# Row sums and pooled products over 128 partitions in a fused attention and MLP kernel

## The chip, the cores and the metric

The kernel runs on one core of one Trainium2 chip. The metric is the device time of one execution in microseconds, the median of three timed runs. The profile comes from a further execution; its span, from the first to the last instruction, is a little shorter than the timed figure. TensorE is called PE, VectorE DVE, ScalarE ACT, GpSimd POOL; SP issues most of the DMA transfers.

## The reference, cut to what matters

Inputs q, k, v are 8 batches x 8 heads x 576 positions x 64 numbers in float32. Each head gets two attentions. One is local: a query sees only keys at a distance under four. The other is pooled: q, k and v are averaged over groups of four positions (144 groups), full attention is computed between groups, and each result is repeated four times. Their sum goes through an MLP.

```python
q_d = q.reshape(B, H, Sd, factor, D).mean(axis=3)      # likewise k_d, v_d; factor 4, Sd 144
out_up = np.repeat(sm_attn(q_d, k_d, v_d), factor, axis=2)
mask = np.abs(pos[:, None] - pos[None, :]) < factor
attn = softmax(np.where(mask, scale * q @ k.T, -1e9))
x = (out_up + attn @ v)                                # to 4608 x 512
h = x @ w_in                                           # 512 x 2048
out = (h * 1 / (1 + exp(-h))) @ w_out                  # 2048 x 512
```

## The kernel before

Heads are worked on in 32 pairs, head h of a pair on partitions 64h to 64h+63. The units of one pair are: T (36 transposes of q and k), S (scores into the PSUM banks AB), exponentials on ACT (Pt local, Pd pooled), Z (row sums by matmuls with 0/1 columns into columns 360 to 431 of the banks CD), a reciprocal on DVE, its spread over partitions (Rb), PV (products with v into CD), the multiplication of PV by Rb into xo, and an addition on POOL into xT. The MLP follows in g1 units (x by w_in, float32, four matmuls of 512 columns, tanh on ACT, a product on DVE) and g2 units (by w_out, bf16).

A list scheduler in the kernel with estimated costs decides the order in which each engine gets its units; a recorder then turns the order into instruction streams with semaphores. So a changed cost or priority can move instructions that the change doesn't touch.

Pairs 0 to 9 are issued as separate units, and for the first eight (NDIR) the reciprocals are spread by PE: split into three bf16 parts, each multiplied by a selector matrix (unit RB). The first eight (NVP) also get their pooled v by matmuls (unit VP); later ones by two POOL additions on an extra copy of v. From n = 10 on, one unit V(n) holds S(n), T(n+1), Z(n-1) and PV(n-2), followed by four g1 and four parts of a g2; there Rb goes through DRAM: scr is written from zr (z) and read back, repeated over 64 partitions (b), all issued from ACT.

```python
NVP = 8; NDIR = 8
# buffers of the first eight pairs lie in gT[1], which the MLP uses later
sel = gT[1][:, 0:2, :]...[:, 0:5, :]                   # 5 selectors 128 x 128
rpart = [gT[1][:, 2 + i, 0:144] for i in range(3)]
zr = sb("zr", [128, 2, 72], F32, 2)

def pe_S(u, p):                                        # 28 matmuls
    ...                                                # 20 local ones, 64x64
    for h in range(2):
        for y in range(2):
            mm(u, AB[half(y), h, 288:432], kd[j][half(h), 64 * y:64 * y + 64], qd[j][half(h), :], rd, [rAB[h]])
    for h in range(2):
        for y in range(2):
            mm(u, AB[half(y), h, 432:504], kd[j][half(h), 128:192], qd[j][half(h), 72 * y:72 * y + 72], rd, [rAB[h]])

def pe_VP(u, p):                                       # 14 matmuls, 64x64, two banks, one wait on itself
    ...

def pe_cross(u, pv, z):                                # products that cross the diagonal of the array
    if pv is not None:
        for h in range(2):
            for j in range(2):
                x = 1 - j
                mm(u, CD[half(h), x, 288:360], vd[n][half(j), 2 * h, :], Pd[m][half(j), h, 72 * x:72 * x + 72],
                   [...], [rCD[x], R(rc)], start=first(x, h), stop=False)
    if z is not None:
        ...                                            # four more, with oh4, into columns 360:432

def pe_main(u, pv, z):
    wait = [R(acc(z if pv is None else pv)[2])]        # the first matmul here waits for pe_cross
    if z is not None:
        for s in range(4):
            for h in range(2):
                for j in range(2):
                    mm(u, CD[half(h), j, 360:432], oh1[half(j), 63 - s:127 - s] if s else ohf[half(j), :],
                       Pt[m][half(j), h, 72 * s:72 * s + 72], [...], [rCD[j]], start=False, stop=False)
        ...                                            # 8 more, from Pd, with oh4 and ohc
    if pv is not None:
        ...                                            # 20 local products and 8 pooled ones, all 64x64

def after_Z(p):
    one("DVE", f"r{p}", 1.2, lambda e: e.reciprocal(zr[i][:, :, :], CD[:, :, 360:432]), r=rCD, ..., prio=-4)
    if p < NDIR:
        # rh on ACT, then rx (subtract), rm (cast), rl (subtract) on DVE: three bf16 parts of 144 columns
        ...
        return
    dma("ACT", f"z{p}", scr[u][:, :], zf, ...)         # 128 x 144 to DRAM
    for h in range(2):
        dma("ACT", f"b{p}", Rb[u][half(h), :], src, ..., r=[R(f"scr{u}")], prio=-5)

def RB(p):                                             # 18 matmuls: 6 column ranges x 3 parts
    for m, x, c, y, e_ in ((0, 0, 0, 0, 144), (1, 0, 144, 0, 144), (2, 0, 288, 0, 72),
                           (2, 1, 0, 72, 144), (3, 1, 72, 0, 144), (4, 1, 216, 0, 144)):
        for a in range(3):
            mm(u, AB[:, x, c:c + e_ - y], sel[:, m, :], rpart[a][:, y:e_], selr + [rpr[a]], [rAB[x]], ...)
    one("ACT", f"eb{p}", 0.85, ...)                    # AB to Rb

def V(n):
    pe_cross(u, pv, z)
    if n < NPAIR: pe_S(u, n)
    if n + 1 < NPAIR: pe_T(u, n + 1)
    pe_main(u, pv, z)
    ...

for n in range(10):
    T(n + 1); feed(); S(n)
    if n > 0: Z(n - 1)
    if n > 1: PV(n - 2); feed()
    if 0 < n <= NDIR: RB(n - 1); VP(n - 1)
    if n > 4: G1((2, 4, 4, 4, 2)[n - 5])
for n in range(10, 46):
    if n < NPAIR + 2: V(n); feed()
    G1(1); g2(part 0); G1(1); g2(part 1); G1(1); g2(part 2); g2(part 3); G1(1)
```

The code above is shortened, with cuts marked by dots and some lines joined.

Of the kernel before, what the change touches and what calls it, by code (L numbers as in the profile page):

```python
# [18 lines left out]
NVP = 8  # L19
NDIR = 8  # L20

# [127 lines left out]
class Unit:  # L149
# [3 lines left out]
                 "ready", "start", "end")  # L153
# [5 lines left out]


class Plan:
# [4 lines left out]
    def __init__(self):  # L166
        self.units = []

    def unit(self, eng, name, cost, prio=None, dcost=0.0):
        u = Unit(eng, name, cost, prio, dcost)  # L170
        u.idx = len(self.units)
        if u.prio is None:
            u.prio = u.idx
        self.units.append(u)
        return u
# [32 lines left out]
    def order(self, look):  # L208
# [12 lines left out]
        while left:  # L221
            best = None
            for e in Prog.ENGS:
                lst = pend[e]
                while head[e] < len(lst) and lst[head[e]] in taken:
                    head[e] += 1
                win = [u for u in lst[head[e]:head[e] + look[e]] if u not in taken and not u.npre]
                if not win:
                    continue
                t = max(free[e], min(u.ready for u in win))  # L230
                c = min((u for u in win if u.ready <= t + 0.05), key=lambda u: (u.prio, u.idx))
                t = max(t, c.ready)
                if best is None or t < best[0]:
                    best = (t, c)
            t, u = best
            u.start = t
            free[u.eng] = t + u.cost
            if u.dcost:
# [4 lines left out]
                u.end = ring[e] + 1.6  # L243
# [15 lines left out]
def bass_hourglass_attn__then__act_silu_kernel(  # L259
# [9 lines left out]
    with kctx:  # L269
# [34 lines left out]
        zr = sb("zr", [128, 2, 72], F32, 2)  # L304
        Rb = sb("Rb", [128, 720], F32, NR)
        xo = sb("xo", [128, 2, 360], F32, NX)
        scr = [nc.dram_tensor(f"scr{i}", [128, 144], F32, kind="Internal").ap() for i in range(NR)]

        sel = gT[1][:, 0:2, :].rearrange("p a (y m) -> p (a y) m", m=128)[:, 0:5, :]
        selr = [R("g1_0"), R("g1_1")]  # L310
        rpart = [gT[1][:, 2 + i, 0:144] for i in range(3)]
        rpr = [R(f"g1_{2 + i}") for i in range(3)]
        rrest = gT[1][:, 5, 0:288].bitcast(F32)
        idn = sb("idn", [128, 64], BF16)
        mask_bf = sb("mask_bf", [128, 288], BF16)
        oh1 = sb("oh1", [128, 127], BF16)
        ohf = sb("ohf", [128, 64], BF16)
        oh4 = sb("oh4", [128, 127], BF16)
        ohc = sb("ohc", [128, 127], BF16)
        pb = sb("pb", [128, 3, 136], BF16)  # L320
# [33 lines left out]
        def constants():  # L354
# [17 lines left out]
            for t, name, val in ((oh1, "oh1", 1.0), (oh4, "oh4", 4.0)):  # L372
                zero(t[:, :], name + "a")
                zero(t[:, 63:64], name, val, 0.07, r=[R(name + "a")])
            zero(ohf[:, :], "ohfa", 1.0)
            zero(ohf[:, 1:5], "ohf", 0.0, 0.07, r=[R("ohfa")])
            zero(ohc[:, :], "ohca")
            for j in range(2):
                zero(ohc[64 * j:64 * j + 16, 63:64], f"ohc{j}", 4.0, 0.07, r=[R("ohca")])
            zero(pb[:, :, :], "pba", cost=0.2)  # L380
            one("DVE", "const", 0.35, lambda e: e.memset(sel[:, :, :], 0.0), w=selr)
# [33 lines left out]
            for j in range(2):  # L415
                one("DVE", "const", 0.1, lambda e, j=j: e.tensor_copy(pb[half(j), :, 58:73], pbs[half(j), j, :, :]),
                    r=[R("cm"), R("pba")], w=[R(f"pb{j}"), R("xo0")])
            for j in range(2):
                one("POOL", "const", 0.5, lambda g, j=j: g.affine_select(
                    out=sel[:, :, half(j)], in_=sel[:, :, half(j)], compare_op=ALU.not_equal, fill=1.0,  # L420
                    base=-64 * j, pattern=[[-1, 5], [0, 64]], channel_multiplier=1), r=selr, w=selr)
# [6 lines left out]
        def load_qk(p):  # L428
            i = p % NQK
            if p == 0:  # L430
                dma("SP", "lkx", Rb[NR - 1][64:128, 0:576], bass.AP(tensor=k.tensor, offset=k.offset,
# [6 lines left out]
            dma("SP", f"lk{p}", qk[i][0:n, 1, :], bass.AP(tensor=k.tensor, offset=k.offset + (128 * p + 64) * 576,  # L438
# [39 lines left out]
        def load_w(c):  # L478
            if c < 4:
                return dma("POOL", f"w{c}", w_in_sb[:, :, 512 * c:512 * c + 512],  # L480
                    moe_w_in[:, 512 * c:512 * c + 512].rearrange("(kc p) f -> p kc f", p=128),
                    [R(f"w_in{c}")], f"w_in{c}", 3.1, cost=0.9)
            else:
                c -= 4
                return dma("POOL", f"w{c + 4}", w_out_bf[:, 4 * c:4 * c + 4, :],
                    moe_w_out[512 * c:512 * c + 512, :].rearrange("(f p) n -> p f n", p=128),
                    [R(f"w_out{c}")], f"w_out{c}", 3.1, cost=0.9)
# [46 lines left out]
        def after_T(p):  # L534
            j = p % NT
            eng = "ACT" if p < NVP else "DVE"
            one(eng, f"eq{p}", 0.68 if p < NVP else 0.72, lambda e: copy(
# [10 lines left out]
            if p >= NVP:  # L548
# [12 lines left out]
        def pe_S(u, p):  # L561
# [10 lines left out]
            for h in range(2):  # L572
                for y in range(2):
                    mm(u, AB[half(y), h, 288:432], kd[j][half(h), 64 * y:64 * y + 64], qd[j][half(h), :], rd, [rAB[h]])
            for h in range(2):
                for y in range(2):
                    mm(u, AB[half(y), h, 432:504], kd[j][half(h), 128:192], qd[j][half(h), 72 * y:72 * y + 72],
                       rd, [rAB[h]])

# [10 lines left out]
        def pe_VP(u, p):  # L590
            n = p % NV

            def pm(o, j, i, c, rk, start, stop, r=(), w=()):
                t = 288 * j + 58 * i
                a = 58 - (t // 4 - 64 * c)
                x = 2 if i == 4 else i % 2
                mm(u, o, pb[half(j), x, a:a + 64], vb[n][half(j), i:i + 6:5, :],
                   [R("pb0"), R("pb1"), R(f"vb{n}")] + list(r), [rk] + list(w), start=start, stop=stop)

            pm(pe_[64:128, 0:128], 0, 4, 1, rE, True, False, w=[R("vpx")])  # L600
            for i in range(5):
                pm(pe_[0:64, 0:128], 0, i, 0, rE, i == 0, i == 4)
            for i in range(4):
                pm(pe_[64:128, 0:128], 1, i, 1, rE, False, i == 3, r=[R("vpx")] if i == 0 else [])
            for h in range(2):
                for i in (3, 4):
                    pm(o0[half(h), 0:128], 1, i, 2, rF, i == 3, i == 4)

        def after_VP(p):
            n = p % NV  # L610
            for s, (t, rk) in enumerate(((pe_, rE), (o0, rF))):
                one("ACT", f"ev{p}", 0.3, lambda e, s=s, t=t: e.activation(
                    vd[n][:, s:4:2, :], t[:, 0:128].rearrange("p (h d) -> p h d", h=2), AF.Copy),
                    r=[rk], w=[R(f"vd{n}{s}")])

        def acc(p):
            return (HP, rH, "crossh") if p < 4 and p % 2 else (CD_, rCD_, "cross")

        def pe_cross(u, pv, z):
# [6 lines left out]

            if pv is not None:
                m, n = pv % NP_, pv % NV
                CD, rCD, rc = acc(pv)
                for h in range(2):  # L630
                    for j in range(2):
                        x = 1 - j
                        mm(u, CD[half(h), x, 288:360], vd[n][half(j), 2 * h, :], Pd[m][half(j), h, 72 * x:72 * x + 72],
                           [R(f"vd{n}0"), R(f"vd{n}1"), R(f"Pd{m}")], [rCD[x], R(rc)], start=first(x, h), stop=False)
            if z is not None:
                m = z % NP_
                CD, rCD, rc = acc(z)
                for h in range(2):
                    for j in range(2):
                        x = 1 - j  # L640
# [303 lines left out]
```

The softmax here doesn't subtract the row's maximum and nothing guards it: scores larger than these inputs give would overflow.

## Time and profile before

| What | Value |
|---|---|
| Time, median of 3 runs | 387.22 us (386.44 to 391.0) |
| Span of the profiled execution | 378.6 us |
| Mean granted PE clock | 0.991 |
| Reciprocals (128 x 144) | 32 of 1.06 us |
| RB matmuls | 144, of 144 or 72 columns |
| Matmuls of T, S, Z, PV for one pair | 36, 28, 28, 32 |
| POOL additions for pooled v | 24 x 1.27 us and 24 x 0.75 us |
| Rb read back from DRAM | 48 transfers of 180 KB, 4.7 us to land |

How to read the profile: a row of tenths gives the busy share of an engine in each of 40 slices of the span. A line of a group ends with the busy time, the mean duration of one in ns, and the idle time just before them with what ended it. A line of waits reads "who, at which line of the kernel, waited for whom: microseconds in total, how many times, the longest". The chain is followed back from the last instruction to what released each step. PE's matmuls overlap, so the distance from one start to the next is of more use than their durations. Line 339 is the helper of nearly all matmuls, L426 that of all DMA issues.

### The profile page before, as it was taken

Reading aid. Unit: us, or ns where it says so; the run is one execution under the profiler, and the core shown is the slowest. Engines: PE = TensorE matmul, PEld = TensorE weight load, DVE = VectorE, ACT = ScalarE, POOL = GpSimd, SP = SyncE. Lnnn points to the kernel's source line nnn. Section 1 sums busy time; section 2 is a strip of 40 time slices with the busy share of each in tenths; the row PEclk is TensorE's granted clock in tenths of the full one; section 3 lists DMA queues with packets and bytes.
Section 4 is the critical chain, followed back from the end, with each engine's and each line's share of the span. In section 5 each row is a group of like instructions: output and inputs, shape, how many; then the busy total and the mean of one; then the engine's idle time right before and its main releaser. Section 6 shows DMA issues by size and latency. Waiting matters only on the chain.

```text
span 378.6 us, 12323 instructions
## 1 busy us (share of the span) xinstructions
PE 338.1 (89%) x5346; PEld 221.3 (58%) x5376; DVE 237.7 (63%) x379; ACT 176.9 (47%) x320; POOL 168.6 (45%) x215
## 2 busy tenths in 40 slices
PE   2475689886999989989999999999999999999996
PEld 1364576654566656656665666666656566666642
DVE  6555468698677858877787776778875434434310
ACT  3635356554355535545544545555543343443421
POOL 6849568367455736665655566555221100000000
PEclk9999999899999999999999999999999999999999
DMA  7999999958978896887887887522222211001012
GB/s 211 280 290 308 244 275 244 237 161 232 257 174 245 220 271 164 222 242 212 223 219 214 213 225 214 162 96 79 84 77 79 66 39 44 28 31 54 28 57 83
DMA packets 77823, 64.37 MB, mean 170 GB/s; under 512 B 47050, under 2 KB 59850, under 8 KB 77770
## 3 DMA queue, kind: packets, MB, share of 16 engines
q1 hardware_dynamic: 66250, 46.68, 45.3%
q10 hardware_dynamic: 7296, 10.62, 10.4%
q0 software_dynamic: 4224, 6.29, 7.7%
q8 instruction: 42, 0.69, 0.8%
q14 instruction: 11, 0.09, 0.1%
HBM read 54.46 MB, written 11.21 MB: 173 GB/s over the span
## 4 chain that ended last, share of the span: by engine, by line
PE 77%; DMA 8%; DVE 4%; SPq 4%; issue 4%; ACT 2%; ACTq 1%; POOL 0%; POOLq 0%
PE HP L339 35%; PE o L339 22%; PE pe_ L339 7%; DMA scr<-zr 6%; PE CD L339 6%; PE AB L339 4%; SPq L426 4%; DMA qk<-in_k_dram 2%; PE o L531 1%; ACTq L426 1%; PE pe_ L531 1%; DVE Pt L586 1%; DVE gT L773 1%; DVE xo L728 1%; DVE gT L699 1%
## 5 line engine op out<-in xcount | busy, mean ns | idle before, releaser
L339 PE MATMUL HP<-xT,w_in_sb 128*128 128x512 f32 x576 | 164.1, 421 | 2.4 <-DVE gT L773 2.4
L773 DVE SCALAR_TENSOR_TENSOR gT<-th,HP 128x512 bf16<-128x512 f32 x144 | 96.4, 683 | 96.9 <-ACT th L771 96.9
L771 ACT ACTIVATE th<-HP 128x512 f32<-128x512 f32 x144 | 85.8, 598 | 84.1 <-PE HP L339 80.5
L339 PEld LDWEIGHTS HP<-xT,w_in_sb 128*128 128x128 f32 x576 | 106.8, 191 | 29.6 <-DVE gT L773 3.1
L339 PE MATMUL o<-w_out_bf,gT 128*128 128x512 bf16 x437 | 102.0, 380 | 1.8
L339 PEld LDWEIGHTS o<-w_out_bf,gT 128*128 128x128 bf16 x464 | 42.1, 98 | 56.1 <-issue 5.7
L755 POOL TENSOR_TENSOR xT<-xo 128x576 fp32r<-128x576 f32 (+3 forms) x48 | 44.4, 938 | 62.7 <-DVE xo L728 62.7
L513 POOL CAST vb<-vs 128x640 bf16<-128x640 f32 x30 | 21.5, 717 | 60.6 <-PE CD L339 52.5
L788 ACT ACTIVATE osb<-o 128x512 f32<-128x512 f32 x29 | 17.3, 597 | 60.9 <-PE o L339 49.7
L690 DVE RECIPROCAL zr<-CD 128x144 f32<-128x144 f32 x30 | 31.7, 1056 | 9.9 <-PE CD L339 5.2
L503 POOL CAST qkb<-qk 128x1152 bf16<-128x1152 f32 x30 | 34.6, 1154 | 3.6 <-PE pe_ L531 2.9
L518 POOL TENSOR_TENSOR vt<-vq 128x512 f32<-128x512 f32 x24 | 30.6, 1274 | 0.2 <-POOL vd L520 0.2
L728 DVE TENSOR_TENSOR xo<-CD,Rb 128x720 f32<-128x720 f32 x30 | 26.8, 895 | 0.0
L339 PE MATMUL pe_<-w_out_bf,gT 128*128 128x512 bf16 x109 | 26.1, 380 | 0.2
L531 PE MATMUL o<-idn,qkb 64*64 64x64 bf16 x576 | 17.6, 206 | 8.8 <-DVE qkb L498 5.6
L545 DVE TENSOR_REDUCE kd<-kT 128x144 bf16<-128x576 bf16 x32 | 23.6, 737 | 0.7 <-ACT kT L541 0.6
L541 ACT ACTIVATE kT<-pe_ 128x576 bf16<-128x576 bf16 x32 | 20.9, 652 | 6.7 <-PE pe_ L531 6.2
L582 ACT ACTIVATE Pt<-AB 128x576 bf16<-128x576 f32 x32 | 20.7, 647 | 6.1 <-PE AB L339 3.8
L531 PEld LDWEIGHTS o<-idn,qkb 64*64 64x64 bf16 x576 | 14.2, 119 | 11.7 <-DVE qkb L498 6.5
L531 PE MATMUL pe_<-idn,qkb 64*64 64x64 bf16 x576 | 17.1, 206 | 1.3 <-DVE qkb L500 0.7
L339 PE MATMUL CD<-Pd,vd 64*64 64x72 bf16 x360 | 15.1, 210 | 3.3 <-DVE xo L728 3.0
L339 PEld LDWEIGHTS pe_<-w_out_bf,gT 128*128 128x128 bf16 x112 | 10.0, 98 | 13.6 <-issue 3.2
(78 smaller groups left out, 350.9 us busy)
## 6 DMA issues: line engine op xcount, KB each, us to landing
vs<-in_v_dram SPq DMA_DIRECT2D x126, 80.0 KB, 4.1
qk<-in_q_dram SPq DMA_DIRECT2D x32, 288.0 KB, 4.9
out_dram<-osb SPq DMA_DIRECT2D x36, 256.0 KB, 2.1
qk<-in_k_dram SPq DMA_DIRECT2D x31, 288.0 KB, 5.7
Rb<-scr ACTq DMA_DIRECT2D x48, 180.0 KB, 4.7
vq<-in_v_dram SPq DMA_DIRECT2D x24, 256.0 KB, 5.9
w_in_sb<-in_moe_w_in_dram POOLq DMA_DIRECT2D x4, 1024.0 KB, 9.9
w_out_bf<-in_moe_w_out_dram POOLq DMA_DIRECT2D x4, 512.0 KB, 8.2
```

Of the source, the lines that this page charges most:

```text
L339: L.op(u, lambda t: t.matmul(out_, lhsT, rhs, start=start, stop=stop, skip_group_check=True), r, w)
L503: one("POOL", f"c{p}", 1.15, lambda g: g.tensor_copy(qkb[j][:, :, :], qk[i][:, :, :]), r=[R(f"qk{i}0"), R(f"qk{i}1")], w=[R(f"qkb{j}0"), R ...
L513: one("POOL", f"cw{p}", 0.72, lambda g: g.tensor_copy(vb[m][:, :, :], vs[i][:, :, :]), r=rr, w=[R(f"vb{m}")])
L518: one("POOL", f"va{p}", 1.3, lambda g: g.tensor_tensor(vt[:, :, :], vq[i][:, :, 0:128], vq[i][:, :, 128:256], ALU.add), r=rr, w=[R("vt")])
L531: L.op(u, lambda e, o=o, w=w, j=j: e.transpose(o, w, idn[half(j), :]), [R("id"), R(f"qkb{n}{x}")], [rE if x else rF])
L541: one("ACT", f"ek{p}", 0.68, lambda e: e.activation(kT[j][:, 3:579].rearrange("p (g r) -> p g r", r=9), pe_[:, 0:288].bitcast(BF16).rearra ...
L545: one("DVE", f"mk{p}", 0.74, lambda e: e.tensor_reduce(kd[j][:, 0:SD], kT[j][:, 3:579].rearrange("p (g r) -> p g r", r=4), AX.X, ALU.add), ...
L690: one("DVE", f"r{p}", 1.2, lambda e: e.reciprocal(zr[i][:, :, :], CD[:, :, 360:432]), r=rCD, w=[R(f"zr{i}")], prio=-4)
L728: one("DVE", f"m{p}", 0.92, lambda e: e.tensor_tensor(xo[x][:, :, :].rearrange("p x (m n) -> p x m n", n=72), CD[:, :, 0:360].rearrange("p ...
L755: one("POOL", f"a{p}", 0.15 + n * 0.0019, lambda g, dst=dst, in0=in0, in1=in1: g.tensor_tensor(dst, in0, in1, ALU.add), r=[R(f"xo{x}")], w ...
L771: one("ACT", f"t{j}_{f}", 0.62, lambda e: e.activation(th[tb][:, :], hps[hb], AF.Tanh, scale=0.5), r=[rH[hb]], w=[R(f"th{tb}")], prio=-1)
L773: one("DVE", f"s{j}_{f}", 0.71, lambda e: e.scalar_tensor_tensor(gT[j % 2][:, f, :], th[tb][:, :], 1.0, hps[hb], ALU.add, ALU.mult), r=[rH ...
```

## The change

The row sums and the pooled part of PV no longer use 64-partition quarters of the array for every product. A matmul now contracts over all 128 partitions at once, with columns that differ between the two halves, so that the row sums of both query halves land on different partitions of one 72-column block: the reciprocal has 72 columns instead of 144. With no products across the diagonal, `pe_cross` and the wait after it go. For the first eight pairs the three bf16 parts lie stacked on partitions (0, 16 and 32 on) by signs that are 0 or -1 for the part in question, so that one selector per block sums the parts, and RB is ten matmuls of 72 columns. VP has seven 128x128 matmuls and is used for 14 pairs. The aim is fewer instructions and shorter steps between the row sums and Rb, and less work for POOL and DMA early on.

```diff
-NVP = 8
+NVP = 14
 NDIR = 8
...
-        zr = sb("zr", [128, 2, 72], F32, 2)
+        zr = sb("zr", [128, 72], F32, 2)
-        scr = [nc.dram_tensor(f"scr{i}", [128, 144], F32, kind="Internal").ap() for i in range(NR)]
+        scr = [nc.dram_tensor(f"scr{i}", [128, 72], F32, kind="Internal").ap() for i in range(NR)]
...
+        rpart = [sb(f"rp{n}", [128, 3, 72], BF16) for n in range(2)]
+        rrest = sb("rrest", [128, 72], F32, 2)
+        sgn = sb("sgn", [128, 2], F32)
...
             for h in range(2):
-                for y in range(2):
-                    mm(u, AB[half(y), h, 288:432], kd[j][half(h), 64 * y:64 * y + 64], qd[j][half(h), :], rd, [rAB[h]])
+                mm(u, AB[:, h, 288:432], kd[j][half(h), 0:128], qd[j][half(h), :], rd, [rAB[h]])
...
+            for i in range(5):
+                mm(u, pe_[:, 0:128], pb[:, 2 if i == 4 else i % 2, a:a + 128], vb[n][:, i:i + 6:5, :], rv, [rE], ...)
+            for i in range(2):
+                mm(u, pe_[:, 128:256], pb2[:, i, :], vb[n][:, 3 + i:9 + i:5, :], rv, [rE], ...)
...
+                for s in range(4):
+                    for h in range(2):
+                        mm(u, CD[half(h), 0, 360:432], ohl[:, 63 - s:127 - s] if s else ohf[:, :],
+                           Pt[m][:, h, 72 * s:72 * s + 72], [...], [rCD[0]], start=first(0, h), stop=False)
+                for y in range(2):
+                    for h in range(2):
+                        mm(u, CD[half(h), 0, 360:432], ohp[:, 59 - 5 * y:123 - 5 * y], Pd[m][:, h, 72 * y:72 * y + 72], ...)
+                for h in range(2):
+                    mm(u, CD[half(h), 0, 360:432], ohe[:, :], Pd[m][:, h, 144:216], ..., stop=True)
...
+                for y in range(2):
+                    for h in range(2):
+                        mm(u, CD[half(h), y, 288:360], vd[n][:, 2 * h, :], Pd[m][:, h, 72 * y:72 * y + 72], ...)
+                # then 4 pooled products and 20 local ones, 64x64
...
+            one("DVE", f"r{p}", 0.56, lambda e: e.reciprocal(zr[i][:, :], CD[:, 0, 360:432]), r=rCD[:1], ..., prio=-400000)
+            dma(eng, f"z{p}", scr[u][0:74, :], zr[i][0:74, :], ..., prio=-500000)
...
         def RB(p):
+            for m in range(10):
+                x, c = divmod(m, 5)
+                mm(u, AB[:, x, 72 * c:72 * c + 72], sel[:, m, :], rpart[p % 2][:, 2, :], ...)
...
         def V(n):
-            pe_cross(u, pv, z)
             if n < NPAIR: pe_S(u, n)
             if n + 1 < NPAIR: pe_T(u, n + 1)
             pe_main(u, pv, z)
```

Besides, the first two transfers of k go through ACT's queue, the eight weight transfers are planned for 16 to 51 us in steps of 5 us (before: 10 to 46), the scheduler assumes 3.2 us instead of 1.6 for an ACT transfer to land, further constants (selectors, signs) are built at the start, and the scheduler has new options that stay unused (an empty list FIRST, a boost of 0). The orders on ACT and DVE differ in places as a result: in the body one more tanh stands between z and b, and in every fourth V the osb eviction comes ahead of b.

## The prediction

> **What bounds the kernel now.** I read the page first, for the total and for how the span divides:
>
> ```profile
> span 378.6 us, 12323 instructions
> PE 338.1 (89%) x5346; PEld 221.3 (58%) x5376; DVE 237.7 (63%) x379; ACT 176.9 (47%) x320; POOL 168.6 (45%) x215
> ...
> PE   2475689886999989989999999999999999999996
> DVE  6555468698677858877787776778875434434310
> ```
>
> The PE row has two regimes. The first quarter is the head, where pairs 0 to 9 go through separate units; after it PE is at 9. The busy time by stretch says how much can be had in each:
>
> ```profile
> 40.00:50.00 10.00, 6.85 (x216) 5.86 (x212) 6.13 (x9) 3.47 (x8) 5.48 (x6) 1.00 1.19 246
> 80.00:100.00 20.00, 15.26 (x305) 10.44 (x306) 17.20 (x25) 8.18 (x14) 13.37 (x14) 0.91 0.84 228
> 180.00:200.00 20.00, 19.86 (x325) 12.65 (x325) 16.19 (x25) 9.60 (x18) 11.71 (x12) 1.00 0.83 215
> 320.00:340.00 20.00, 19.89 (x89) 12.48 (x90) 7.57 (x11) 7.89 (x14) 0.00 (x0) 1.00 0.07 27
> ```
>
> Columns are PE, PEld, DVE, ACT, POOL busy, then clock, DMA share and GB/s. After 100 us only fewer PE microseconds help. In the head PE is idle a third of the time, and late in it DVE is at 17.2 of 20. On the timeline S(1) starts at 15.6, S(6) at 57.0 and V(10) at 92.2: an iteration takes (57.0-15.6)/5 = 8.3 us, then (92.2-57.0)/4 = 8.8 us. The waits of the first 100 us tell what lies between:
>
> ```profile
> ACT Rb L718 <- PE AB L339: 14.5, 8, 4.7
> PEld AB L339 <- issue: 5.9, 6, 2.6
> PEld AB L339 <- DVE gT L699: 3.7, 3, 1.6
> PEld CD L339 <- DVE xo L728: 3.4, 1, 3.4
> ```
>
> ACT waits for the broadcast RB, RB for the last split part (L699), that for reciprocal and casts; S of the next pair needs RB's banks AB. It is a loop through PE, DVE and ACT, not one full engine. "Issue" is PE waiting for nothing shown; the chain through the head has it in large pieces:
>
> ```profile
> 24.56 1.29 issue
> ...
> 31.02 2.44 issue
> ...
> 44.65 2.61 issue
> ...
> 65.71 1.52 issue
> ```
>
> In the DMA records, packets of the instruction queue (42 on the page, 0.69 MB, so 16 KB each) start at 23.43, 30.80, 44.49 and 64.83 us, just ahead of these: PE is out of instructions. 5376 matmuls each with a weight load over 42 packets make 256 per packet.
>
> In the body one V unit reads so:
>
> ```profile
> 113.47 0.19 PE L531 MATMUL pe_<-idn,qkb 64*64 64x64 bf16 x1
> 113.64 0.23 PE L339 MATMUL CD<-Pt,ohf 64*64 64x72 bf16 x4
> ...
> 114.18 0.73 PE L339 MATMUL HP<-xT,w_in_sb 128*128 128x512 f32 x2
> ```
>
> There is a hole of 0.17 us between T's last transpose and the first row sum: `pe_main` waits by semaphore for `pe_cross`. The unit spans 112.83 to 114.18. Lastly the chain in the body:
>
> ```profile
> 160.30 4.42 DMA scr<-zr
> 165.23 0.61 ACTq L426
> 166.23 0.61 ACT osb L788
> ```
>
> ACT stands at the issue of the Rb read until scr has landed; behind it in the stream waits the osb eviction, and T(19) waits for that bank. V(18) lasts 2.2 us from first to last matmul start, against 1.1 mostly.
>
> [...] four 64x64 matmuls start every 32 ns together (the 36 transposes take 0.28 us), and V enters about 0.1 us after the 128x128 stream ends, and leaves likewise. [...]
>
> **The change by parts, head.** Of an early iteration (pairs 1 to 5) and a late one (6 to 9):
>
> - Reciprocal: 30+2 of 1.056 us on 144 columns, now 72. Half plus a small fixed share: 0.56 (an estimate). -0.50.
> - Split: the three DVE steps take at least 0.30, 0.23 and 0.31 us on the timeline; half the columns leaves about 0.6 of 0.84. -0.2.
> - RB: 18 matmuls, 2160 columns, 1.7 to 1.9 us early and about 0.97 late on the timeline. Now ten of 72: a third of the columns, but a weight load each, so I take 0.65 and 0.45. -1.1, -0.5.
> - VP: 14 small matmuls become 7 of 128x128, equal in time; two ACT evictions of 0.28 become one near 0.4. -0.15.
> - Fetch: T 36 + S 28 + Z 28 + PV 32 + RB 18 + VP 14 = 156 matmuls become 36+26+14+28+10+7 = 121, 22% fewer blocks. The trace has about 14 us of such stalls over the ten iterations; a quarter less is 0.3 to 0.4 each. -0.4, -0.2.
> - Mode changes: Z and part of PV are 128x64, part of S is 64x128, VP is 128x128: two to four more at 0.1. +0.3.
>
> Sums are -2.05 early and -1.25 late. Not all lies on the loop: early, casts wait for loads (cast 6 starts at 36.5, its k landed at 36.2), late DVE still has its s operations. I count three quarters: 5 x 1.55 + 4 x 0.95 = 11.5 us. V(10) waited 3.4 us at its very start for xo, because `pe_cross` came first; now S and T go ahead of that wait: -1. Against it, the new constants (the selector's copy of 1280 columns on DVE, mask work, all POOL constants before mq0) stand ahead of the first casts; moving lkx and lk0 to ACT's queue gives some back. +1.5. The head: **-11**.
>
> **The change by parts, body and tail.** Row sums were 7 groups of four 64x64, now 7 pairs of 128x64; PV's coarse part 3 groups of four, now two pairs and one group. The array time is therefore equal though 20 of 124 matmuls go. Removed: the hole, 0.13 us beyond a normal 32 ns step. Added: modes go 64x64, 64x128, 64x64, 128x64, 64x64, four changes more, at 0.05 (within the small modes, a guess) to 0.1. Net -0.1 to +0.2, I take +0.08; by 24 units **+2**. VP of pairs 9 to 13 falls here: 5 x 7 matmuls of 128 columns near 60 ns, **+2.2**; the POOL additions it replaces (1.27 + 0.75 us a pair) were off the path, as were 6 pairs of vq loads, except as early DMA relief. The shorter reciprocal gives DVE 12 us in the body, but DVE isn't the bound. What does move: z is issued earlier, one more tanh stands between z and b in ACT's stream, and in every fourth V the osb eviction now precedes b. The stalls of that kind are V(18) 1.1, V(22) 0.9, V(26) 0.3, the V(14) to V(15) period 1.6 over the others, and V(10) to V(11) 11.9 against 8.75, so 3: 6.9, of which I give 4.5 back. **-4.5**. After 300 us nothing changes: **0**.
>
> Sum: -11 + 2 + 2.2 - 4.5 = -11.3; 387.2 - 11.3 = **375.9 us**.
>
> **Rivals.** (1) The head is bound by loads. For it: up to 36 us the casts start as loads land, and the DMA share is above 1. Against: cast 8 starts 8 us after its k landed, and the weights (6.3 MB) and vq now come later. Then the head gives 4 and the time is about 383. (2) Mode changes cost 0.1 to 0.15 each in every V: six instead of two, +0.4 less 0.13, so +6.5 in the body instead of +2, and more in the head: 381 to 384. For it: both visible changes cost 0.1. (3) The head loop shortens fully and fetch stalls nearly vanish, as blocks are used more slowly: 6 us more, 370. For it: stalls of 2.5 us stand right on the chain. [...]
>
> **Range and chances.** The terms are uncertain by 5 (head), 4 (modes), 2 (ACT stalls), 2 (startup): about 7 together. 366 to 384.5. The 2% line is 379.5, 3.6 below which the middle lies: faster 0.66, same 0.28, slower 0.06.
>
> **What would show it.** V(10) starts near 81 instead of 92.2; reciprocals at 0.56; RB at or below 0.65; fewer "issue" pieces before 90 us; no hole after T but short ones at each mode change, V still at 1.35 to 1.45 us; no DMA scr ahead of the osb eviction on the chain; 300 us to the end unchanged in length. Wrong would be: V above 1.6 (rival 2), V(10) after 88 with casts on DMA waits (rival 1), or 128x64 pairs that don't run two at a time, which would add 0.3 a unit.

## The result, and the profile after

| | Time, median | Range |
|---|---|---|
| Before | 387.50 us | 386.44 to 391.0, 4 executions |
| After | 367.37 us | 366.79 to 370.98, 4 executions |

The ratio is 0.949, with a 95% interval of 0.942 to 0.956: 20 us less. The prediction was 375.9 us, 366 to 384.5; the result lies in the range, near its fast end, and 8.5 us below the middle.

The four executions of before in this table lie at the upper end of what that kernel does: 48 others, taken beside the variants on four chips, took 379.94 to 391.89 us, with a median of 385.4. An execution more than 1.5% above the fastest of its kernel counts as slow: without the slow ones the median of before is 384.1 us over the four chips, and of the variants below that of `a_act16` is 372.1, of `a_t2` 380.1, of `a_rb3` 373.3 and of `a_best` 362.6. Against 384.1 the gain of after is 16.7 us, a ratio of 0.957; this is the fairer figure, and the one to hold the parts against.

One more caution for everything read from the two traces: the profiled execution of after was its longest (370.98 us, span 369.2), while that of before took 380.31 us (span 378.6), shorter than the executions beside it. The two traces are therefore only 9.4 us apart. Stages are compared in the traces, totals by the medians.

The page of after, its span, busy times and rows of tenths for PE and DVE:

```profile
span 369.2 us, 10834 instructions
...
PE 340.1 (92%) x4658; PEld 219.0 (59%) x4658; DVE 224.1 (61%) x390; ACT 178.0 (48%) x318; POOL 156.7 (42%) x203
...
PE   1684799889799999999999999999999999999996
...
DVE  7574889877456677776777767777755343433400
```

718 of 5376 matmuls are gone. The first quarter of the PE row, 2475689886 before, is now 1684799889. The same four stretches as before (columns PE, PEld, DVE, ACT, POOL, clock, DMA share, GB/s):

```profile
40.00:50.00 10.00, 7.98 (x162) 6.14 (x160) 9.00 (x14) 5.54 (x11) 8.76 (x12) 0.59 1.26 309
80.00:100.00 20.00, 17.51 (x275) 11.38 (x274) 11.07 (x19) 8.63 (x18) 6.60 (x10) 0.98 1.08 254
180.00:200.00 20.00, 20.00 (x332) 12.86 (x335) 13.27 (x21) 10.63 (x19) 10.55 (x13) 1.00 0.78 226
320.00:340.00 20.00, 20.00 (x91) 12.12 (x90) 8.16 (x12) 8.95 (x15) 0.00 (x0) 1.00 0.10 39
```

From 80 to 100 us DVE is down from 17.2 to 11.1 of 20, and by then the body has begun. In the body PE is full before and after. The waits of the first 100 us:

```profile
PEld o L568 <- POOL qkb L540: 8.3, 4, 4.2
...
POOL qkb L540 <- DMA qk<-in_k_dram: 6.8, 2, 6.4
...
PEld AB L358 <- issue: 2.5, 9, 0.4
...
ACT Rb L726 <- PE AB L358: 1.6, 3, 0.8
...
PEld AB L358 <- DVE rp L705: 1.6, 3, 0.7
```

ACT's wait for the broadcast RB, 14.5 us in eight waits before, is 1.6 in three. "Issue" of S and RB is 2.5 instead of 5.9, and no single one is over 0.4 us. (A second trace of before has 2.5 us there too, but with single ones of 1.5; its wait for the broadcast RB is 16.1 us.) First among PE's waits now stands that of the transposes for POOL's cast, and POOL waits for the load of k. The chain through the head says the same; its large pieces of "issue" have gone, and a load has come in their place:

```profile
18.98 9.87 DMA qk<-in_k_dram
...
28.96 1.16 POOL qkb L540
...
66.26 0.16 issue
```

That last line is the longest "issue" piece from 10 to 90 us. The V unit of the body, on the timeline (start, duration, what):

```profile
172.51 0.38 PE L358 MATMUL AB<-qd,kd 64*64 64x72 bf16 x6
172.82 0.21 PE L568 MATMUL o<-idn,qkb 64*64 64x64 bf16 x1
...
173.10 0.19 PE L568 MATMUL pe_<-idn,qkb 64*64 64x64 bf16 x1
173.22 0.22 PE L358 MATMUL CD<-Pt,ohf 128*64 128x72 bf16 x2
173.28 0.27 PE L358 MATMUL CD<-Pt,ohl 128*64 128x72 bf16 x6
173.38 0.23 PE L358 MATMUL CD<-Pd,ohp 128*64 128x72 bf16 x4
...
173.69 0.33 PE L358 MATMUL CD<-Pt,vb 64*64 64x58 bf16 x20
173.95 0.96 PE L358 MATMUL HP<-xT,w_in_sb 128*128 128x512 f32 x3
```

Between the last transpose (173.10) and the first row sum (173.22) lie 0.12 us, no longer a wait but a change of mode. The six products of `ohl`, three pairs, take 0.10 us, 33 ns a pair: two 128x64 matmuls do run at a time. The unit lasts 1.49 us from first to last start, 1.12 before. From 98 us on the chain between V units is PE alone, with no DMA scr, and no osb but the last one at 366 us:

```profile
99.39 2.08 PE HP L358 x4
101.46 0.77 PE pe_ L358 x7
102.23 1.28 PE HP L358 x4
```

(The 0.77 us of seven matmuls is VP of one of the pairs 9 to 13; the other four of them take about 0.4 us each.) Ahead of that the old stall is still on the chain, twice:

```profile
78.18 6.06 DMA scr<-zr
...
85.53 0.60 ACT osb L791
...
88.49 7.87 DMA scr<-zr
...
97.52 0.61 ACT osb L791
...
98.17 0.21 PE o L568
```

ACT stands at the issue of the Rb read until scr has landed, osb waits behind it, and T(13) waits for osb. Time by stages, from the first matmul of each unit; the third and fourth columns are two experiments, explained below:

| Stage | Before | After | New products, old planning | Old products, new planning |
|---|---|---|---|---|
| to S(1) | 15.7 | 14.6 | 17.4 | 15.8 |
| S(1) to V(10) | 76.5 | 59.3 | 61.6 | 72.5 |
| V(10) to V(14) | 37.1 | 44.2 | 41.5 | 37.5 |
| V(14) to V(30) | 141.5 | 144.0 | 144.1 | 141.1 |
| V(30) to the end | 107.8 | 107.1 | 108.0 | 106.8 |
| Sum | 378.6 | 369.2 | 372.6 | 373.6 |

So the head gave 18.3 us and the body took some back: 7.1 before V(14) and 2.5 after it. Of the 7.1, 4.3 are one long step from V(12) to V(13), 13.6 us against 9.2 to 9.4 in most variants below: there the write of scr took 7.9 us to land, and T(13) waited 2.6 us for osb as shown above (in `a_wide`, with the same order of units, the read could follow the write after 3.8 us). Another 0.9 is one g1 unit that after does ahead of V(14) and before does later (33 g1 units ahead of V(14) against 32, and 97 against 96 ahead of V(30)); it also makes the last stage look shorter.

### The profile page after: what moved, and what is told of

Same layout as the page of the kernel before. It is cut to its first block, busy times and chain, and to the rows that moved or that the text cites. A ratio compares the mean times of both kernels' runs of the same rounds, so it can differ in the third digit from the quotient of the medians.

```text
span 369.2 us, 10834 instructions
## 1 busy us (share of the span) xinstructions
PE 340.1 (92%) x4658; PEld 219.0 (59%) x4658; DVE 224.1 (61%) x390; ACT 178.0 (48%) x318; POOL 156.7 (42%) x203
## 4 chain that ended last, share of the span: by engine, by line
PE 78%; DMA 8%; DVE 8%; POOL 2%; ACT 2%; ACTq 1%; issue 1%; POOLq 0%; DVEq 0%
PE HP L358 34%; PE o L358 25%; PE pe_ L358 8%; DMA scr<-zr 5%; PE CD L358 5%; PE AB L358 4%; DMA qk<-in_k_dram 3%; PE o L568 2%; POOL xo L381 2%; DVE rrest L702 1%; DVE gT L776 1%; DVE xo L736 1%; ACTq L463 1%; DVE rp L705 1%; DVE kd L582 1%
## 5 line engine op out<-in xcount | busy, mean ns | idle before, releaser
L358 PEld LDWEIGHTS HP<-xT,w_in_sb 128*128 128x128 f32 x576 | 107.1, 192 | 27.6 <-DVE rp L705 1.1
L358 PE MATMUL o<-w_out_bf,gT 128*128 128x512 bf16 x464 | 107.2, 380 | 0.0
L568 PE MATMUL o<-idn,qkb 64*64 64x64 bf16 x576 | 17.4, 205 | 17.0 <-POOL qkb L540 7.5
L568 PEld LDWEIGHTS o<-idn,qkb 64*64 64x64 bf16 x576 | 13.3, 117 | 20.6 <-POOL qkb L540 8.3
L555 POOL TENSOR_TENSOR vt<-vq 128x512 f32<-128x512 f32 x18 | 22.9, 1272 | 4.7 <-DMA vq<-in_v_dram 4.7
L708 DVE RECIPROCAL zr<-CD 128x72 f32<-128x72 f32 x24 | 14.6, 607 | 8.4 <-PE CD L358 8.4
L568 PE MATMUL pe_<-idn,qkb 64*64 64x64 bf16 x576 | 16.7, 205 | 1.6 <-DVE qkb L537 1.0
L358 PEld LDWEIGHTS pe_<-w_out_bf,gT 128*128 128x128 bf16 x112 | 10.0, 98 | 13.6 <-issue 3.2
L586 DVE TENSOR_REDUCE qd<-qT 128x144 bf16<-128x576 bf16 x24 | 17.8, 743 | 0.0
```

The costliest lines, as they stand in the source:

```text
L358: L.op(u, lambda t: t.matmul(out_, lhsT, rhs, start=start, stop=stop, skip_group_check=True), r, w)
L555: one("POOL", f"va{p}", 1.3, lambda g: g.tensor_tensor(vt[:, :, :], vq[i][:, :, 0:128], vq[i][:, :, 128:256], ALU.add), r=rr, w=[R("vt")])
L568: L.op(u, lambda e, o=o, w=w, j=j: e.transpose(o, w, idn[half(j), :]), [R("id"), R(f"qkb{n}{x}")], [rE if x else rF])
```

## The experiments

The theory: (a) the head got faster because the loop through RB, the split and S lost array time and instructions, (b) instruction supply in the head eased far more than the predicted 3 us, (c) four added mode changes cost about 0.1 us each in every V, and (d) the new planning (the order of loads and of ACT's queue) has a share of its own. The rivals: the planning alone does it all; or the gain is the shorter reciprocal; or PE's array time in the head, or its clock, not the number of instructions. Every ratio is to runs of the kernel before on the same chip. Except where the text says otherwise each variant keeps the order of units of after on all engines.

### The kernel before, once more

> The kernel before, unchanged, to see how much its time and its trace vary. The gain of the timed runs is 20 us, that of the two profiles 9.4 us (378.6 to 369.2), so about 10 us must lie in differences between executions. Theory A: the kernel before has executions of 380 and of 387 to 391 us, the first profile was one of the short ones, and a second profile differs from it in the head (0 to 100 us) by instruction-fetch gaps or late loads. Theory B: the first profile is typical and the timed runs are longer in a way that no profile shows. A says a second profile with V(10) starting anywhere from 90 to 100 us and a span that follows it; B says a span of 378 to 379 again.

Measured: 383.75 us (380.21 to 391.06, 20 executions; 385.73 for those compared with), ratio 0.9985 (0.9948 to 1.0022). A second trace has V(10) at 91.6, V(14) at 130.0 and its end at 380.8. The two traces are only 2.2 us apart, 0.5 of it at V(10), but both are of short executions, so what the long ones lose stays unseen. All gaps of type issue ahead of PE's loads from 10 us to V(10) come to 17.7 us in the first trace and 12.5 in the second: a difference of a few us in such a sum says nothing.

### Taking the planning and the products apart

`a_oldsched` gives after's products the planning of before:

```diff
-u.end = ring[e] + (3.2 if e == "ACT" else 1.6)
+u.end = ring[e] + 1.6
-ek = "ACT" if p < 1 else "SP"          # and lkx back from ACT to SP
+ek = "SP"
-    load_w(c).ready = 16.0 + 5.0 * c
+    load_w(c).ready = (10, 14, 18, 22, 34, 38, 42, 46)[c]
-after_Z(z); after_PV(pv)               # and no rule that a v load follows its qk load
+after_PV(pv); after_Z(z)
```

`b_newsched` is the reverse: the kernel before with these planning changes of after and nothing else. Both change the order of units. The raised priorities of the reciprocal, the split, the Rb transfers and the addition into xT, which are also part of the change, go with the products in both runs; their share was not taken apart.

> The kernel after with the old planning: first k transfers on SP, weights planned from 10 to 46 us, 1.6 us assumed for an ACT transfer, multiplication unit listed ahead of the reciprocal, the rule on the order of v loads gone. The array work is that of the kernel after. Theory L (the computation itself, shorter steps and fewer instructions, gives the head's gain): 367 to 372 us. Theory S (the planning of loads and of ACT's transfers gives half or more of it): 375 to 380 us.

> The kernel before with the new planning alone: first k transfers on ACT, weights planned from 16 to 51 us, 3.2 us assumed for an ACT transfer to land, reciprocal listed ahead of the multiplication, v loads only after their q and k. The array work is that of the kernel before. If planning is a gain of its own: 7 to 8 us below before (taking it out of the kernel after cost 7.7 us), a ratio of 0.98, with V(10) 3 to 5 us earlier than 92. If it gains only together with the shorter steps: within 2 us of before.

Measured: new products with old planning 375.05 us (374.4 to 377.78), ratio 0.975 (0.968 to 0.982), at the edge of what theory S expected. Old products with new planning 375.47 us (375.3 to 376.08), ratio 0.980 (0.973 to 0.986), as expected of planning as a gain of its own. Either half is worth about 2 to 2.5%, and the product of the two ratios, 0.955, is close to the 0.957 of both. In the stage table the products give 13.2 us at V(10) (79.0 against 92.2), the planning 4.0 (88.2), both 18.3 (73.9). With old products the large pieces of issue stay on the chain of the head under the new planning:

```profile
28.85 1.16 issue
...
35.09 2.09 issue
...
42.37 2.17 issue
...
49.78 2.62 issue
```

The two runs also bear on where the osb stalls went. The step from V(14) to V(30) is 144.1 with old planning and 144.0 with new: in the trace of `a_oldsched` every V from V(11) on lasts 1.49 us, though ACT still issues the Rb read ahead of osb:

```profile
163.30 1.11 ACTq L463 DMA_DIRECT2D Rb<-scr  x2
164.46 0.60 ACT L774 ACTIVATE th<-HP 128x512 f32<-128x512 f32 x1 [2.85 <-PE HP L358]
165.07 0.60 ACT L791 ACTIVATE osb<-o 128x512 f32<-128x512 f32 x1
```

There z was issued at 159.19, after a reciprocal of 0.61 us, and the read 4.1 us later; osb is done at 165.67, and V(19) starts at 165.83 and doesn't stall. So the stalls can go without the new planning. That the shorter reciprocal removes them isn't shown: V(18), V(22) and V(26) of before stall after a short step with three g1 units (7.66 us from V(17) to V(18)), and `a_oldsched` has no such step from V(18) on (9.02 us from V(18) to V(19)), so the place of the g1 units is a rival. With old products and new planning osb stands ahead of the read, V(18) falls from 2.20 to 1.21 us, yet V(14) to V(30) is only 0.4 shorter, as it holds one g1 unit more (0.9 us) and one V period grew (9.07 where 8.55 is usual).

`a_act16` changes one planning constant of after:

```diff
-u.end = ring[e] + (3.2 if e == "ACT" else 1.6)
+u.end = ring[e] + 1.6
```

> The kernel after, with the scheduler's assumption for an ACT transfer put back from 3.2 to 1.6 us, the rest of the planning kept. It puts the Rb read ahead of the osb eviction in ACT's stream again in every fourth V. If this is most of what the planning gives: 371 to 374 us, with V(18), V(22), V(26) standing 0.3 to 1.1 us at T for osb. If the loads' order and the weights' times give most: 367 to 369.

Measured: 372.79 us (368.11 to 375.34), ratio 0.967 (0.957 to 0.977), some 5 us above after; single executions overlap, and against the 0.957 of after the interval isn't clear. The profiled execution was its shortest, at 368.11; in it V(18), V(22) and V(26) last 1.49 us each, so the expected stalls are not there. This one constant moves units on PE, DVE and POOL too, not only on ACT. It may be worth some 5 us; by which wait its longer executions lose them no trace shows.

### Instructions or array time in the head

`a_t2` does the 36 transposes of each of pairs 0 to 10 twice, `a_wide` adds three idle matmuls of 224 columns to T instead:

```diff
 pe_T(u, p)
+pe_T(u, p)                                            # a_t2
+for _ in range(3):                                    # a_wide
+    mm(u, o0[0:64, 288:512], qkb[...][0:64, 0, 0:64], qkb[...][0:64, 0, 0:224], ...)
```

> The kernel after, with the transposes of pairs 0 to 10 done twice: 36 matmuls more per head iteration, so again about 157 matmuls in each, at 0.28 us of array time. Order unchanged. Fetch theory (the number of PE instructions in the head sets part of its time): PE gaps of type issue of 1 to 2.6 us come back, at least 6 us in sum against 2.5 now, V(10) 5 to 7 us later, 372 to 374. Rival (issue gaps went away because PE now waits for other things in the same places): at most the array time, 11 x 0.28 = 3 us, 367 to 370.

> The kernel after, with three idle matmuls of 224 columns added to T of pairs 0 to 10: 0.28 us of array time in each, as in the run with the transposes done twice, but 3 matmuls instead of 36. Order unchanged. Fetch theory: the 16 us that the doubled transposes cost were instructions, not array time, so issue gaps stay near 2.5 us, V(10) within 3 us of 73.9 and the time 367 to 371. Rival (the head cannot take 0.28 us more of PE per iteration without losing its places in the loop): V(10) after 82 and above 377.

Measured: `a_t2` 383.58 us (378.48 to 385.52), no interval given, median of before beside it 384.12: most of the gain is gone, 12.7 us of it by the medians given with the result. `a_wide` 368.18 us (366.94 to 372.47), ratio 0.958 (0.950 to 0.966), 0.8 above after. V(10) starts at 87.2 with doubled transposes and at 73.8 with the idle matmuls. The chain of `a_t2` in the head again has what before had:

```profile
14.63 1.23 issue
...
40.39 1.44 issue
...
45.81 3.03 issue
...
67.24 1.87 issue
...
72.07 3.89 issue
```

Packets of the instruction queue start at 39.33, 45.80 and 66.58 us, ahead of three of these. The waits of the first 90 us have it too: 8.4 us of issue ahead of CD, 5.1 ahead of AB.

The two loads on the array are about equal: from its first weight load to the next unit's first matmul an early T takes 0.63 us in after, 1.11 in `a_t2` and 1.18 in `a_wide`, so that each adds at most some 6 us over eleven T. What differs is the 396 matmuls more of `a_t2`, each with its weight load, against 33. The number of instructions in the head is what costs; a little array time in T is hidden, in waits for casts. Cautions: issue gaps differ between executions of one kernel, 17.7 and 12.5 us in the two traces of before. By my sum over the trace, all gaps over 0.2 us ahead of PE's weight loads from 10 us to V(10) are 33.6 us before (issue 17.7), 21.0 after (issue 2.5), 26.6 in `a_t2` (issue 16.5) and 18.1 in `a_wide` (issue 6.6, not the 2.5 expected, with pieces of 1.5 and 2.3 us on the chain). Nor is the count of instructions the only thing that sets them: `a_vp8` below, with no more matmuls in its head than after, has 10.9 us of issue, and its V(10) is 2.2 us later.

PE's clock is a rival here. In after T has these two forms (columns PE, PEld, POOL busy with T, clock, DMA share, GB/s):

```profile
36.50:37.90 1.40, 0.48 (x36) 0.37 (x36) 0.00 (x0) 1.00 1.31 325
41.90:43.00 1.10, 0.70 (x36) 0.56 (x36) 0.00 (x0) 0.50 1.19 294
```

Its transposes start 8 ns apart at full clock and 13 at half (36 in 0.28 and in 0.46 us). Ahead of the first record of the clock, at 52.1 us before and 34.5 in after, they are 13 ns apart too, so the 1.00 that the views print there isn't to be trusted. With that stretch counted as half, PE has half its clock for 55 us up to V(10) before, 45 in after, 61 in `a_t2` and 43 in `a_wide`. But in `a_recip2` below it is 49, with V(10) only 0.4 us later than in after, and in `a_rb3` 40, with V(10) 9.6 later: the clock doesn't set V(10) by itself. What share of the loss of `a_t2` it has stays open.

### The reciprocal and RB by themselves

`a_recip2` does every reciprocal twice (the first into a spare tile). `a_rb3` does each RB matmul three times, 30 of 72 columns, so 2160 columns as before.

```diff
+L.op(ur, lambda e: e.reciprocal(zx[i][:, :], CD[:, 0, 360:432]), ...)     # a_recip2
-for m in range(10):
+for m in [m for m in range(10) for _ in range(3)]:                        # a_rb3
```

> The kernel after, with every reciprocal done twice (the first into a spare tile): 1.2 us of DVE per pair between row sums and split or scr, about what the 144 columns took before. The order of all engines' streams is unchanged. Theory C (the loop from row sums to Rb sets the head's pace): 0.6 us more in each of about nine head iterations at three quarters, V(10) 4 us later, time 371 to 372. Theory N (the reciprocal lies beside loads and PE work): under 1.5 us, 367 to 369. In the body nothing in either.

> The kernel after, with each of RB's ten matmuls done three times: 30 matmuls, 2160 columns, as many columns as before. Order unchanged. Theory C: 0.7 to 1.2 us more per RB on the loop, eight times at three quarters, plus the 160 matmuls more to fetch: V(10) 5 to 7 us later, 373 to 375. Theory N: the time rises by under 2 us, 367 to 369.5.

Measured: `a_recip2` 369.37 us (366.92 to 370.55), ratio 0.963 (0.955 to 0.970): 2.0 us more than after for 32 x 0.61 = 19 us more on DVE, with single executions overlapping. V(10) is at 74.2, 0.4 later: nearer theory N than C. `a_rb3` 373.63 us (369.02 to 376.11), ratio 0.971 (0.960 to 0.980): 6 us more, V(10) at 83.5, 9.6 later, in the trace of its longest execution, for 7.5 us more of RB and 160 more matmuls. Here the array time, or the instructions with it, is not hidden. The two causes within RB weren't separated: 6 us over 160 matmuls are 37 ns for each, 12.7 over the 396 of `a_t2` are 32, so the count alone could explain both.

### Mode changes

`a_s64` puts the pooled scores of S back into four 64x64 matmuls (two mode changes fewer in V); `a_order` besides puts all 64x64 products of PV ahead of the 128x64 ones of Z and PV (one more fewer: three changes with entry and exit, against six).

```diff
-for h in range(2):                                                        # a_s64
-    mm(u, AB[:, h, 288:432], kd[j][half(h), 0:128], qd[j][half(h), :], rd, [rAB[h]])
+for h in range(2):
+    for y in range(2):
+        mm(u, AB[half(y), h, 288:432], kd[j][half(h), 64 * y:64 * y + 64], qd[j][half(h), :], rd, [rAB[h]])
```

> The kernel after, with the pooled scores in S put back from two 64x128 matmuls to four 64x64 ones: two mode changes fewer in each V, two matmuls more. Theory of the mode changes (0.1 us each, V(20) of the kernel after lasts 1.49 us from first to last matmul start, against 1.12 before): V falls to about 1.29 us, 22 units give 4.4 us in the body, the time is about 363. Rival, that the number of instructions is what counts: V stays near 1.49 and the time does not fall.

> As the run with the pooled scores back in 64x64, and PV's 64x64 products put ahead of the 128x64 ones of Z and PV, so that V goes 128x128, 64x64, 128x64, 128x128: three mode changes instead of six. Mode-change theory: V near 1.15 to 1.2 us from first to last start, 22 x 0.3 = 6.6 us and the same order of saving per pair in the head, 359 to 361 us. Rival: row sums come later in V, the chain to Rb gets 0.3 us longer and DVE or ACT stalls eat the gain; 366 to 368.

Measured: `a_s64` 362.48 us (360.47 to 363.02), ratio 0.939 (0.933 to 0.945); `a_order` 363.02 us (360.65 to 365.58), 0.941 (0.934 to 0.949). No execution of either is as long as the shortest of after (366.79). The first is as the mode-change theory expected, the second 2 us longer. On the timeline of `a_s64` the first transpose starts 0.10 us after the first pooled score, 0.31 in after:

```profile
167.23 0.27 PE L358 MATMUL AB<-qd,kd 64*64 64x72 bf16 x8
167.33 0.19 PE L568 MATMUL o<-idn,qkb 64*64 64x64 bf16 x1
```

In `a_order` the local products follow the last transpose (167.25) without a hole, and from the last group of 64x64 products to the first row sum it is 0.15 us:

```profile
167.27 0.34 PE L358 MATMUL CD<-Pt,vb 64*64 64x58 bf16 x20
167.43 0.22 PE L358 MATMUL CD<-Pd,vd 64*64 64x72 bf16 x4
167.58 0.22 PE L358 MATMUL CD<-Pt,ohf 128*64 128x72 bf16 x2
```

V lasts 1.49, 1.27 and 1.15 us with four, two and one changes inside it. The three lie on a line: 1.04 plus 0.11 a change. The mean step from V(17) to V(29) is 8.98, 8.74 and 8.68 us. That `a_order` isn't faster than `a_s64` in all goes with single long V units in its trace (V(13) 1.86, V(15) 1.72 us, V(11) to V(14) 28.2 against 27.4).

`a_best` keeps the 64x128 scores in the head (p < 10), for fewer instructions there, and takes `a_order` from V(10) on:

```diff
+if p < 10:
+    for h in range(2):
+        mm(u, AB[:, h, 288:432], kd[j][half(h), 0:128], qd[j][half(h), :], rd, [rAB[h]])
+    return
```

> Both findings put together: in the head (pairs 0 to 9) the pooled scores stay in two 64x128 matmuls, as in the kernel after, for fewer instructions; in V they are four 64x64 ones, and PV's 64x64 products go ahead of the 128x64 ones, for three mode changes instead of six. If instructions in the head and mode changes in the body are the two prices: 360 to 362.5 us, at or just under the two runs with the pooled scores in 64x64 (362.5 and 363.0), V(20) at 1.15 us. If the two matmuls per head pair do not matter: 362 to 363.

Measured: 364.43 us (359.17 to 367.49, 6 executions), ratio 0.943 (0.934 to 0.951). That is longer than expected. V(10) starts at 72.6, earlier than in any other, but the step from V(12) to V(13) is long again (13.8 us), here with an issue gap of 2.9 us in it. It can't be told from `a_s64`; the best median found is that of `a_s64`.

### Eight pairs with pooled v on PE instead of 14

```diff
-NVP = 14
+NVP = 8
```

> The kernel after, with pooled v on PE for 8 pairs as before, on POOL for pairs 8 to 13 again. If its worth is the relief of POOL and DMA in the head and around V(10) to V(13): 2 to 5 us slower than after, 369 to 372, with later casts from pair 8 on. If its cost in the body (five VP of 0.6 us) outweighs: 2 to 3 us faster, 364 to 366.

This changes the order of units. Measured: 370.47 us (367.75 to 372.24), ratio 0.963 (0.954 to 0.971), 3.1 above after, executions overlapping. V(10) to V(11) takes 16.1 us, 11.9 in after. The chain of this variant there:

```profile
70.16 8.45 DMA vq<-in_v_dram
...
78.83 1.28 POOL vt L555
...
81.57 1.18 POOL xT L760
...
82.79 2.50 PE HP L358 x5
```

POOL stands before the additions of pooled v until vq has landed (8.4 us in five waits from 72 to 102 us), the addition into xT comes behind them in its stream, and g1 on PE waits for xT (3.1 us). After has POOL vt waiting 4.7 us once in its first 100 us.

## Why the prediction was right, and where not

**The head, predicted -11, measured -18.3.** The direction was right. Predicted without the startup were -12.5 (11.5 and 1), and with old planning S(1) to V(10) is 14.9 shorter; the difference of the rest is the planning, which the prediction gave no gain of its own in the head beyond the startup. Term by term:

- Reciprocal, predicted 0.56 and -0.50. It takes 607 ns, -0.45, as the groups on the page of after show (busy time, mean ns, idle before):

```profile
L708 DVE RECIPROCAL zr<-CD 128x72 f32<-128x72 f32 x24 | 14.6, 607 | 8.4 <-PE CD L358 8.4
```

  Three quarters of it was put on the loop. Three quarters of the 0.61 us that doubling adds would be 4.1 us over nine iterations; it costs 0.4 at V(10) and 2.0 in all, so in after's head most of it lies beside the path.
- Split, predicted -0.2. It did not shrink: means of 371, 604 and 696 ns before, and of 859, 270 and 645 after, 0.1 more in sum. Two of the steps are now a multiplication by a sign and an addition in one. The shortest of each step took 0.30, 0.22 and 0.31 us before and 0.28, 0.18 and 0.28 after, so half the columns saved 0.1, not 0.2, and the means are far above these minima in both kernels. From the groups of after's first 75 us:

```profile
L702 DVE SCALAR_TENSOR_TENSOR rrest<-rp,sgn,zr 128x72 f32<-128x72 bf16 x8 | 6.9, 859 | 0.2 <-ACT rp L700 0.2
...
L705 DVE SCALAR_TENSOR_TENSOR rp<-rp,sgn,rrest 128x72 bf16<-128x72 bf16 x8 | 5.2, 645 | 0.1
```

- RB, predicted at 0.65 early and 0.45 late: 0.53 and 0.30 from first to last start (1.66 and 0.89 before). The difference between early and late goes with the clock: RB of after took 0.53 at 38.4 and 44.6 us, where 0.50 was granted, and 0.30 at 50.8, at 1.00. ACT's wait for RB, 14.5 us before and 1.6 after, says that it lay on the loop, and `a_rb3` agrees, but neither settles it: `a_best` has 6.9 us of that wait and the earliest V(10), and added instructions would explain `a_rb3` too.
- VP, predicted equal in time but for its evictions, -0.15: from first to last start it takes 0.61 early and 0.35 late (7 matmuls, 107 and 56 ns apart), where the 14 took 0.90 and 0.59; one eviction of 0.38 stands where two of 0.28 stood.
- Fetch, predicted -0.4 and -0.2 an iteration, 3 us in sum, is the term that was most mis-sized. "Issue" gaps fell by 15.2 (17.7 to 2.5; by 10 from the second trace of before), 8.3 of it (to 9.4) with the products alone; part came back as waits for casts, so that all gaps fell by 12.6 (by 5.9 with the products alone). An iteration has 35 matmuls fewer; 36 put back into each as transposes cost 12.7 us, 13.3 at V(10). This was rival 3. I had counted stalls in proportion to the instructions; removing 22% of them removed most of the stall in this trace.
- Startup, predicted +1.5: S(1) came 1.1 earlier. With old planning it came 1.7 later. Over all variants with the new planning it lies between 14.5 and 16.4, so neither is resolved.

**Mode changes in the body, predicted +0.08 a V and +2.** Measured +0.39 (8.58 to 8.97 us, the regular period), 6.2 us over V(14) to V(30) and about 9 over 24 units. The step that failed is "at 0.05 (within the small modes, a guess)": a change between the smaller modes costs 0.11 us, about what the one into 128x128 takes (0.12), so four of them cost 0.45, less the 0.1 that V had to lose at `pe_cross`. This was the size of rival 2. In the V of after shown above the starts on both sides of the changes lie 0.13 us apart (into 64x128), 0.16 (out of it, after products of 144 columns), 0.12 (into 128x64), 0.13 (out of it) and 0.12 (into 128x128): no kind of change is cheaper there.

**VP for 14 pairs, predicted +2.2.** The five VP take 2.3 us (four of 0.4 and one of 0.73 to the next matmul), as predicted. But the variant with eight pairs is 3.1 slower rather than faster, though executions overlap, and its chain shows why: what I called "off the path" (the POOL additions) was not, as the wait for vq reached g1 through xT. So the net was probably a gain.

**ACT stalls, predicted -4.5.** From V(14) on they vanish: every V of after lasts 1.49 us there, and V(14) to V(30) grew by 2.5 where mode changes alone give 6.2, so 3.7 came back. The cause that I gave, osb ahead of the read in ACT's stream, isn't needed: under old planning, without that order, they vanish too. What removes them there stays open; an earlier end of the reciprocal and another place of the g1 units are both possible. The 3 us that I put on V(10) to V(11) did not come back in after's trace (11.9 us in both), and the step from V(12) to V(13) lost 4.3 us to a stall of just this kind.

**The tail, predicted 0:** -0.7, which is the one g1 unit done earlier. **Rival 1** (loads bound the head) is what is left now: a load of k on the chain for 9.9 us, and casts as the largest wait of PE. It did not hold the gain down to 4.

**The sum.** -11.3 was predicted and -20 measured, -16.7 against the fairer base. The planning accounts for about 8 of it (375.05 less 367.37; 384.1 less 375.47), of which I had counted only the stalls; instruction supply for more than was counted; mode changes took back some 7 more than was counted. Large errors of both signs met in the range, so that the sum came out as well as it did is partly luck.

What stays open: why executions of before vary between 380 and 391 us while with new planning alone they lie within 0.8 us of each other; which wait the planning constant for ACT removes; and why one write of scr took 7.9 us to land in the trace of after, so that V(12) to V(13) became long, and not in most variants with the same order of units.

## What to carry to other kernels

Where PE runs through many small matmuls while loads fill the DMA queues (a DMA share of 1.04 to 1.29 from 10 to 70 us of before), count instructions, not only array time: 36 more matmuls in each of eleven units cost 12.7 us here, three wide ones 0.8. The wider contraction saved instructions and no array time in V: even sorted by mode, V takes 1.15 us against 1.12 before. Its changes of mode cost 0.11 us each, so sort products by mode before merging any. And when a change comes with a new schedule, run the new schedule on the old work too: here it was about half of the gain.

## What the runs showed of the hardware that was not expected

- A change of tile mode on PE cost about 0.11 us, between 64x64, 64x128 and 128x64 as well (V of 1.49, 1.27 and 1.15 us with four, two and one changes inside).
- The reciprocal of float32 from PSUM on 128 partitions took 1056 ns for 144 columns and 607 for 72: by a straight line through the two, an estimate, 6.2 ns a column and 0.16 us fixed.
- The first split step on DVE, one operation of three operands on 72 columns, took 0.86 us in the mean (singly 0.28 to 2.41); the plain subtraction on 144 columns before took 0.37 (0.30 to 0.76).
- The granted clock of PE was 0.59 in after from 40 to 50 us, where PE was busy 8.0 of 10 us. The 1.00 of before there comes from no record: its first one starts at 52.1 us, and up to then its transposes are 13 ns apart, as at half clock in after.
- T, the same 36 transposes, took 0.46 us from first to last start at half clock and ahead of the first record of the clock, and 0.28 at full clock, in both kernels; RB and VP of after likewise took 0.53 against 0.30 and 0.61 against 0.35.
